# The small blocks' gathers, scatters and summing matmul on 128 rows instead of 32

## The chip, the cores and the metric

The kernel runs on one core of a Trainium2 chip. The metric is the device time of one execution in microseconds. The profile is of one further execution.

## The reference

Three layers follow one another. The first is a linear recurrence over 768 time steps: for each of 4 batches and 8 heads a complex state of 48 x 48 is multiplied by a normalised decay, a key-value product is added, and a query reads it. Its output, seen as 3072 tokens of 384 numbers, goes through a dense layer, and then through a layer of 8 experts, of which each token takes one:

```
h = max(max(x @ w1, x @ w2), x @ w3);  x1 = h @ w_out            # dense layer
expert_idx = argmax(cosine(x1, expert_emb) / tau)                # router
out[mask] = gate[mask] * (max(x1[mask] @ w1[e], 0) @ w2[e])      # mask: the tokens of expert e
```

## The kernel before

Phase 1 (up to about 593 us) computes the recurrence and the dense layer in 12 units of 256 tokens, from a recorded list of operations that a planner in the kernel (class `Recorder`) orders; its lines all appear as L299. The dense layer's output rows go to `x1d` in HBM, from which phase 2 fetches them by token number.

Phase 2 is the expert layer, and the change lies in it. Tokens of one expert are packed into blocks of 128 rows. A column of `self.src` (one number for each of 128 partitions) holds the token numbers of a block, a column of `self.dst` the output rows, a column of `self.gate_of` the gates. Where a row of a block is empty, `late_route` (L1141 to L1145) writes 0 into `src` and 4096 into `dst`; a scatter is told that only rows below 3072 exist (`bounds_check`). The main loop of `phase2` goes over `STEPS`, 14 of them (two single blocks, then 11 pairs of blocks and one more single one, 25 blocks in all). A step k does, in program order: the gather of the rows of step k+2 (L1174), the loads of the next step's expert weights on SP's queue (L1168, L1169), their splitting into a high and a low part by ACT and DVE (`prep`, L1195 to L1205), the two halves of the first matmul (`mm1`, L1243; ACT and DVE evict into `hhi` and `hlo`, L1247 and L1248), the next step's transposes (L1220 to L1226), the second matmul (`mm2`, L1259), the gated copy to `yo` (L1263) and the scatter of each block to `out` (L1265).

An expert with few tokens left over gets a small block of at most 32 rows (`MT`). There are 5 of them (`MINI`), woven into five of the steps (`WITH`) by the generator `small`. A small block loads its weights (L1279, L1280), gathers its 32 rows (L1282), transposes them (L1288), computes the hidden layer in four quarters laid out over 4 x 32 output partitions (L1295), and after the second matmul (L1310) has four partial sums on partitions 0 to 31, 32 to 63, 64 to 95 and 96 to 127. One matmul with `self.four` adds them (L1315): `four` is 128 x 32 and has a one where the partition's number modulo 32 is the column's. ACT applies the gates (L1317) and GpSimd scatters 32 rows (L1318).

```
1282  g.indirect_dma_start(out=xg[:MT], ..., in_offset=IndirectOffsetOnAxis(ap=self.src[:MT, i:i + 1], axis=0), ...)
1315  t.matmul(ps[:MT], self.four, part, start=True, stop=True)
1317  s.activation(y[:MT], ps[:MT], AF.Copy, scale=self.gate_of[:MT, i:i + 1])
1318  g.indirect_dma_start(out=self.io["out"], in_=y[:MT], ..., ap=self.dst[:MT, i - KE:i - KE + 1], ...)
1346  self.four = pool.tile([128, MT], F32, name="four")
1347  nc.vector.tensor_reduce(self.four, self.ident.rearrange("p (j r) -> p r j", r=MT), axis=AX.X, op=ALU.add)
```

`four` is made on DVE before the first step of the loop. `self.mask` is a 128 x 128 tile of phase 1 (the causal mask of the recurrence, read at L594); phase 2 reads it once more, at L856, in the routing of the last tokens. That routing, `late_route`, is written into step 1 (`LATE`), runs on DVE for the most part and ends with `src` and `dst` of all later blocks (L1142, L1145) and with some flags (L1417 to L1425). The gathers of the blocks from step 4 on, and of all small blocks, need its `src`.

In phase 2 the framework, not the kernel, orders the instructions of each engine at compile time, by their place in the program, by what they wait for, and by its own estimate of times. Each engine then runs its queue in that order. An indirect DMA is issued by GpSimd (POOL in the profile).

Of the kernel before, what the change touches and what calls it, by code (L numbers as in the profile page):

```python
# [9 lines left out]
F32 = mybir.dt.float32  # L10
# [4 lines left out]
AF = mybir.ActivationFunctionType  # L15
ALU = mybir.AluOpType
AX = mybir.AxisListType
# [21 lines left out]
KE, KP = 2 * PE, 2 * (PE + PL)  # L39
NBLK = KP + SG  # L40
MT, MINI = 32, 5
# [272 lines left out]
class Prog:  # L314
# [954 lines left out]
    def small(self, pool, mp, pg, m):  # L1269


        nc = self.nc
        t, v, s, g = nc.tensor, nc.vector, nc.scalar, nc.gpsimd
        i, KD, KF, Q = NBLK + m, DM // 128, FF2 // 128, FF2 // 4
        e = nc.values_load(self.mtab[0:1, m:m + 1], engines=[ET.SP], min_val=0, max_val=E - 1,
                           skip_runtime_bounds_check_because="a count of 8 comparisons, of which one fails")
        w1 = mp.tile([128, KD, FF2], F32, tag="w1m", bufs=1, name=f"w1m{m}")
        w2 = mp.tile([128, KF, DM], F32, tag="w2m", bufs=1, name=f"w2m{m}")
        nc.sync.dma_start(w1, self.io["w21"][bass.ds(e, 1)].rearrange("a p (k f) -> p (a k) f", f=FF2))  # L1279
        nc.sync.dma_start(w2, self.io["w22"][bass.ds(e, 1)].rearrange("a p (k f) -> p (a k) f", f=DM))  # L1280
        xg = pool.tile([128, DM], F32, tag="xg", bufs=4, name=f"xgm{m}")
        g.indirect_dma_start(out=xg[:MT], out_offset=None, in_=self.x1d,  # L1282
                             in_offset=bass.IndirectOffsetOnAxis(ap=self.src[:MT, i:i + 1], axis=0),
                             bounds_check=NT - 1, oob_is_err=False)
        yield
        px = pg.tile([128, KD, MT], F32, tag="px", bufs=2, name=f"pxm{m}")
        for k in range(KD):
            t.transpose(px[:, k], xg[:MT, k * 128:(k + 1) * 128], self.ident[:MT, :MT])  # L1288
        x = pool.tile([128, KD, MT], F32, tag="xT", bufs=2, name=f"xm{m}")
        s.copy(x, px)  # L1290
        yield
        ph = pg.tile([128, Q], F32, tag="ph", bufs=3, name=f"phm{m}")
        for k in range(KD):
            for j in range(4):
                t.matmul(ph[j * MT:(j + 1) * MT], x[:, k], w1[:, k, j * Q:(j + 1) * Q], start=k == 0, stop=k == KD - 1,  # L1295
                         skip_group_check=True)
        h = mp.tile([128, Q], F32, tag="hm", bufs=1, name=f"hm{m}")
        s.activation(h, ph, AF.Relu)
        yield
        pt = pg.tile([128, 2, 128], F32, tag="px", bufs=2, name=f"pt{m}")  # L1300
        for c in range(2):
            t.transpose(pt[:, c], h[:, c * 128:(c + 1) * 128], self.ident)
        hT = mp.tile([128, 2, 128], F32, tag="hT", bufs=1, name=f"hT{m}")
        v.tensor_copy(hT, pt)
        yield
        py = pg.tile([128, DM], F32, tag="py", bufs=2, name=f"pym{m}")
        for c in range(2):
            for j in range(4):
                r = slice(j * MT, (j + 1) * MT)
                t.matmul(py[r], hT[:, c, r], w2[:, 2 * j + c], start=c == 0, stop=c == 1, skip_group_check=True)  # L1310
        part = pool.tile([128, DM], F32, tag="yo", bufs=3, name=f"part{m}")
        s.copy(part, py)
        yield
        ps = pg.tile([128, DM], F32, tag="py", bufs=2, name=f"psm{m}")
        t.matmul(ps[:MT], self.four, part, start=True, stop=True)  # L1315
        y = pool.tile([128, DM], F32, tag="yo", bufs=3, name=f"ym{m}")
        s.activation(y[:MT], ps[:MT], AF.Copy, scale=self.gate_of[:MT, i:i + 1])  # L1317
        g.indirect_dma_start(out=self.io["out"], in_=y[:MT], in_offset=None,  # L1318
                             out_offset=bass.IndirectOffsetOnAxis(ap=self.dst[:MT, i - KE:i - KE + 1], axis=0),
                             bounds_check=NT - 1, oob_is_err=False)  # L1320
        yield

    def phase2(self):
        tc, nc = self.tc, self.nc
        with ExitStack() as ctx:
            regs = tc.queue_regs(depth=QD, engines=[ET.SP, ET.Activation, ET.DVE], name="wr")
            qp = ctx.enter_context(tc.tile_pool(name="wq", bufs=1, reuse_waits="tile"))
            q1 = qp.queue([128, 3072], F32, regs=regs, name="q1", contiguous=True)
            q2 = qp.queue([128, 3072], F32, regs=regs, name="q2", contiguous=True)
            pg = ctx.enter_context(tc.tile_pool(name="pg2", bufs=2, space=PSUM, reuse_waits="tile"))  # L1330
            pool = ctx.enter_context(tc.tile_pool(name="m2", bufs=1, reuse_waits="tile"))
            wq = ctx.enter_context(tc.tile_pool(name="ws", bufs=1, reuse_waits="tile"))

            late_ctx = ctx.enter_context(ExitStack())
            rp = late_ctx.enter_context(tc.tile_pool(name="rtp", bufs=1, reuse_waits="tile"))
            load, gather, prep, share, transpose, mm1, mm2, st = self.moe2(pool, wq, pg, regs, q1, q2)
            late = self.late_route(rp, pg)
            gather(*STEPS[1])
            load(0)
            first = prep(*STEPS[0])  # L1340
            for _ in range(2):
                next(first)
            last = NS - SPARE
            few = iter(())

            self.four = pool.tile([128, MT], F32, name="four")
            nc.vector.tensor_reduce(self.four, self.ident.rearrange("p (j r) -> p r j", r=MT), axis=AX.X, op=ALU.add)
            for k, (i, n) in enumerate(STEPS[:last]):
                if k + 2 < last:
                    gather(*STEPS[k + 2])  # L1350
                p, after = iter(()), k + 1 < last
                if k == 0:

                    share(*STEPS[:2])
                    p = first
                elif after:
                    load(k + 1)
                    p = prep(*STEPS[k + 1])
                if k + 1 in WITH:

                    small = self.small(pool, mp, pg, WITH.index(k + 1))
                    next(small)
                next(p, 0)
                mm1(i, n, 0)

                for _ in few:
                    pass
                if k in WITH:
                    few = small_now
                    next(few)  # L1370
                if k + 1 in WITH:
                    small_now = small
                next(p, 0)
                mm1(i, n, 1)
                next(few, 0)
                next(p, 0)
                if after:
                    transpose(*STEPS[k + 1])
                for b in range(n):
                    next(p, 0)  # L1380
                    mm2(i, n, b)
                    next(few, 0)
                for _ in p:
                    pass
                for _ in range(LATE.count(k)):
                    next(late)
                if k == LATE[-1]:
                    late_ctx.close()
                    mp = ctx.enter_context(tc.tile_pool(name="mp", bufs=1, reuse_waits="tile"))

    def run(self):
# [287 lines left out]
```

## Time and profile before

| what | us |
|---|---|
| median of 3 runs | 886.02 |
| lowest, highest | 885.44, 891.13 |
| profiled execution | 888.17 |
| its span in the trace | 886.4 |

The span is what lies between the first and the last instruction of the trace; 1.77 us of the profiled execution lie around it. All stretches and times below are in us from the span's start. Busy shares are those of one engine; PE is TensorE's matmuls, PEld its weight loads, which overlap them.

### The profile page before, as it was taken

The page shows a single profiled execution, that of the slowest core. Times are in us where ns is not written, and L with a number is a line of the kernel's source. Part 1 is how long each engine was busy: PE and PEld are TensorE (multiplying, and loading weights), DVE is VectorE, ACT ScalarE, POOL GpSimd, SP SyncE. Part 2 cuts the span into 40 slices and gives each one's busy share as a digit, 9 for nine tenths or more (in the row PEclk, how much of TensorE's full clock was granted, in tenths as well). Part 3 has the DMA queues.
Part 4 walks back from the last instruction along what each step waited for, and adds up shares of the span by engine and source line. Part 5 has one row for each costly group of instructions (what it writes and reads, how often), then busy time and mean ns, then how long its engine had stood idle before and what let it go on. Part 6 is the DMA issues. An engine that isn't in the chain of part 4 may idle for free. (4 is left out here: it accounts for less than half of the span.)

```text
span 886.4 us, 17517 instructions
## 1 busy us (share of the span) xinstructions
PE 812.3 (92%) x6741; PEld 710.8 (80%) x6741; DVE 643.4 (73%) x1371; ACT 434.6 (49%) x918; POOL 124.1 (14%) x194
## 2 busy tenths in 40 slices
PE   0877999999999999999999999998969899989991
PEld 0755697979898887979797988888959788888991
DVE  5998898899888899889898853548966454555610
ACT  7897545435554436454445341137327455455420
POOL 5521100010000000000001000021032222222110
PEclk9889899999999999999999999999989999999996
DMA  8641153443716071715254250050065756665000
GB/s 309 252 116 28 38 133 92 98 130 60 171 31 165 25 175 36 154 51 138 89 101 112 47 109 4 19 206 25 21 251 199 295 205 251 246 251 180 14 20 21
DMA packets 38669, 107.93 MB, mean 122 GB/s; under 512 B 5299, under 2 KB 26833, under 8 KB 35504
## 3 DMA queue, kind: packets, MB, share of 16 engines
q1 hardware_dynamic: 30032, 77.15, 30.6%
q0 software_dynamic: 8000, 28.78, 9.8%
q8 instruction: 55, 0.90, 0.4%
q10 hardware_dynamic: 544, 0.79, 0.3%
q14 instruction: 38, 0.31, 0.1%
HBM read 97.19 MB, written 9.88 MB: 121 GB/s over the span
## 5 line engine op out<-in xcount | busy, mean ns | idle before, releaser
L299 PE MATMUL ph<-xhi,whi 128*128 128x256 f32 x648 | 117.2, 289 | 0.4 <-DVE slotgate L299 0.4
L299 PE MATMUL ph<-xhi,wlo 128*128 128x256 f32 x648 | 112.9, 283 | 0.0
L299 PE MATMUL ph<-xlo,whi 128*128 128x256 f32 x648 | 112.9, 283 | 0.0
L299 PEld LDWEIGHTS ph<-xhi,whi 128*128 128x128 f32 x648 | 93.5, 192 | 2.9 <-PE slots L299 0.5
L299 PEld LDWEIGHTS ph<-xlo,whi 128*128 128x128 f32 x648 | 93.2, 192 | 0.0
L299 PEld LDWEIGHTS ph<-xhi,wlo 128*128 128x128 f32 x648 | 93.1, 192 | 0.0
L1243 PE MATMUL ph<-xh,w1s 128*128 128x256 f32 x264 | 76.2, 289 | 1.6 <-DVE hlo L1248 1.6
L1205 DVE TENSOR_TENSOR w2l<-queue_q_buf,w2h 128x768 fp32r<-128x768 f32 x52 | 47.8, 954 | 37.2 <-ACT w2h L1204 36.9
L1243 PE MATMUL ph<-xh,w1l 128*128 128x256 f32 x264 | 74.7, 283 | 0.0
L1243 PE MATMUL ph<-xl,w1s 128*128 128x256 f32 x264 | 74.6, 283 | 0.0
L1259 PE MATMUL py<-w2h,hhi 128*128 128x384 f32 x200 | 69.8, 349 | 4.7 <-ACT hhi L1247 4.7
L1259 PE MATMUL py<-w2h,hlo 128*128 128x384 f32 x200 | 68.8, 345 | 5.1 <-DVE hlo L1248 4.9
L299 PE MATMUL px<-wo,h 128*128 128x392 f32 x192 | 71.2, 502 | 0.0
L1248 DVE SCALAR_TENSOR_TENSOR hlo<-ph,hhi 128x512 fp32r<-128x512 f32 x50 | 34.3, 686 | 48.7 <-ACT hhi L1247 48.7
L1259 PE MATMUL py<-w2l,hhi 128*128 128x384 f32 x200 | 68.3, 341 | 0.0
L299 DVE TENSOR_TENSOR h<-ph,h 128x512 f32<-128x512 f32 x72 | 49.5, 688 | 25.1 <-PE ph L299 22.9
L299 PE MATMUL py<-at,v 128*64 128x128 f32 (+1 forms) x576 | 57.1, 279 | 0.4 <-DVE at L299 0.4
L299 PE MATMUL pa<-S 112*128 112x128 f32 x384 | 52.6, 280 | 4.8 <-ACT kt L299 4.8
L299 PEld LDWEIGHTS pa<-S 112*128 112x128 f32 x384 | 49.3, 194 | 9.7 <-ACT kt L299 5.5
L1243 PEld LDWEIGHTS ph<-xh,w1s 128*128 128x128 f32 x264 | 50.5, 191 | 7.0 <-issue 5.0
L1247 ACT ACTIVATE hhi<-ph 128x512 fp32r<-128x512 f32 x50 | 29.7, 598 | 49.7 <-PE ph L1243 49.5
L299 PE MATMUL py<-S,Ts 112*64 112x128 f32 x480 | 51.5, 291 | 0.0
(404 smaller groups left out, 1832.3 us busy)
## 6 DMA issues: line engine op xcount, KB each, us to landing
queue_q_buf<-w SPq DMA_DIRECT2D x26, 1536.0 KB
S<-QK SPq DMA_DIRECT2D x46, 289.1 KB
QKr<-qk SPq DMA_DIRECT2D x11, 768.0 KB
X<-a SPq DMA_DIRECT2D x10, 768.0 KB
w1m<-w SPq DMA_DIRECT2D x5, 1536.0 KB
w2m<-w SPq DMA_DIRECT2D x5, 1536.0 KB
v<-v POOLq DMA_DIRECT2D x24, 288.0 KB
x1d<-x1s SPq DMA_DIRECT2D x20, 192.0 KB
```

The source lines that it names most:

```text
L299: getattr(getattr(self.nc, c[0]), c[1])(*c[2], **c[3])
L1205: v.tensor_sub(lo, bv[:, c], hi.bitcast(F32))
L1243: t.matmul(ph[:, f], a, b, start=o == 0, stop=o == len(ops) - 1)
L1247: s.activation(hi, ph, AF.Relu).ins,
L1248: v.scalar_tensor_tensor(lo, ph, 0.0, hi.bitcast(F32), op0=ALU.max, op1=ALU.subtract).ins]
L1259: t.matmul(py, a[:, f, r], c[:, k % 4], start=o == 0, stop=o == 3 * KF - 1)
```

## The change

The gather and the scatter of a small block take all 128 rows of their index column instead of the first 32, and so does the gated copy between them. For that, the summing matmul yields 128 rows: `four` becomes 128 x 128, with zeros in its columns 32 to 127. It has no tile of its own any more: it lies in `self.mask`, which GpSimd sets to zero after the late routing's second part in step 1, and of which DVE then fills columns 0 to 31 by the same reduction as before. The reduction ahead of the loop and the 128 x 32 tile go.

```diff
-        g.indirect_dma_start(out=xg[:MT], out_offset=None, in_=self.x1d,
-                             in_offset=bass.IndirectOffsetOnAxis(ap=self.src[:MT, i:i + 1], axis=0),
+        g.indirect_dma_start(out=xg, out_offset=None, in_=self.x1d,
+                             in_offset=bass.IndirectOffsetOnAxis(ap=self.src[:, i:i + 1], axis=0),
                              bounds_check=NT - 1, oob_is_err=False)
...
-        t.matmul(ps[:MT], self.four, part, start=True, stop=True)
+        t.matmul(ps, self.four, part, start=True, stop=True)
         y = pool.tile([128, DM], F32, tag="yo", bufs=3, name=f"ym{m}")
-        s.activation(y[:MT], ps[:MT], AF.Copy, scale=self.gate_of[:MT, i:i + 1])
-        g.indirect_dma_start(out=self.io["out"], in_=y[:MT], in_offset=None,
-                             out_offset=bass.IndirectOffsetOnAxis(ap=self.dst[:MT, i - KE:i - KE + 1], axis=0),
+        s.activation(y, ps, AF.Copy, scale=self.gate_of[:, i:i + 1])
+        g.indirect_dma_start(out=self.io["out"], in_=y, in_offset=None,
+                             out_offset=bass.IndirectOffsetOnAxis(ap=self.dst[:, i - KE:i - KE + 1], axis=0),
                              bounds_check=NT - 1, oob_is_err=False)
...
-            self.four = pool.tile([128, MT], F32, name="four")
-            nc.vector.tensor_reduce(self.four, self.ident.rearrange("p (j r) -> p r j", r=MT), axis=AX.X, op=ALU.add)
...
                 if k == LATE[-1]:
                     late_ctx.close()
+                    self.four = self.mask
+                    nc.gpsimd.memset(self.four, 0.0)
+                    nc.vector.tensor_reduce(self.four[:, :MT], self.ident.rearrange("p (j r) -> p r j", r=MT), axis=AX.X,
+                                            op=ALU.add)
```

## Rows read from the trace of the kernel before

**Rows 1.** Part 1 of the page, busy us, share of the span, instructions

```profile
PE 812.3 (92%) x6741; PEld 710.8 (80%) x6741; DVE 643.4 (73%) x1371; ACT 434.6 (49%) x918; POOL 124.1 (14%) x194
```

**Rows 2.** Three stretches: length, PE, PEld, DVE, ACT, POOL busy, clock, DMA share, GB/s

```profile
606.00:651.00 45.00, 43.23 (x329) 42.40 (x327) 39.40 (x118) 21.36 (x31) 4.00 (x4) 1.00 0.07 22
651.00:664.00 13.00, 6.03 (x27) 5.20 (x28) 6.08 (x19) 0.96 (x2) 6.85 (x6) 0.74 0.98 406
664.00:869.00 205.00, 196.72 (x1453) 178.72 (x1451) 97.72 (x115) 99.61 (x150) 46.80 (x44) 1.00 0.49 181
```

**Rows 3.** Timeline of PE: start, duration, instruction, idle before it and its releaser

```profile
660.40 0.90 PE L1220 MATMUL pxg<-ident,xg 128*128 128x128 f32 x3 [6.80 <-DMA xg<-x1d,srcrow]
```

**Rows 4.** Timeline of POOL, 618 to 742 us

```profile
618.57 1.00 POOL L1265 DMA_INDIRECT out<-yo,srcrow  x1 [8.92 <-ACT yo L1263]
...
652.30 2.16 POOL L1174 DMA_INDIRECT xg<-x1d,srcrow  x1 [14.47 <-DVE dstrow L1145]
...
740.56 0.96 POOL L1282 DMA_INDIRECT xgm<-x1d,srcrow  x1 [0.30 <-PE py L1259]
```

**Rows 5.** Four lines' own views, indirect DMAs on POOL: ns min/median/max, first and last start

```profile
L1282 POOL DMA_INDIRECT xgm<-x1d,srcrow x5: 920/952/1907, 661.6 to 820.2; - x5
L1174 POOL DMA_INDIRECT xg<-x1d,srcrow x24: 1006/1032/2502, 577.0 to 801.0; - x24
L1318 POOL DMA_INDIRECT out<-ym,dstrow x5: 882/894/900, 695.3 to 856.1; - x5
L1265 POOL DMA_INDIRECT out<-yo,dstrow x19: 982/1000/1623, 684.0 to 869.7; - x19
```

**Rows 6.** Page part 3, bytes moved in HBM

```profile
HBM read 97.19 MB, written 9.88 MB: 121 GB/s over the span
```

**Rows 7.** Chain that ended last, in time: start, us, what (DMA: issue to landing)

```profile
849.45 2.59 DMA out<-yo,dstrow
...
856.08 3.16 DMA out<-ym,dstrow
...
864.81 4.12 DMA out<-yo,dstrow
```

**Rows 8.** Timeline of PE, 738 to 750 us

```profile
746.96 0.37 PE L1288 MATMUL pxm<-ident,xgm 32*128 32x32 f32 x3
```

**Rows 9.** Groups by line and form, 575 to 887 us: busy us, mean ns, idle before

```profile
L299 PE MATMUL px<-wo,h 128*128 128x392 f32 x16 | 5.4, 492 | 0.0
...
L1315 PE MATMUL psm<-part,four 128*32 128x384 f32 x10 | 4.2, 498 | 0.0
...
L299 PEld LDWEIGHTS px<-wo,h 128*128 128x128 f32 x16 | 3.0, 190 | 1.9
...
L1315 PEld LDWEIGHTS psm<-part,four 128*32 128x32 f32 x10 | 0.7, 107 | 0.7
```

**Rows 10.** The same view: the gated copies on ACT

```profile
L1263 ACT ACTIVATE yo<-py,slotgate 128x384 f32<-128x384 f32 x25 | 14.6, 582 | 46.4 <-PE py L1259 38.4 <-issue 6.3 <-ACT w2h L1204 1.6
...
L1317 ACT ACTIVATE ym<-psm,slotgate 32x384 f32<-32x384 f32 x5 | 2.9, 573 | 0.8 <-PE psm L1315 0.8
```

**Rows 11.** Timeline of DVE, 580 to 662 us

```profile
580.21 0.39 DVE L1347 TENSOR_REDUCE four<-ident 128x32 f32<-128x128 f32 x1 [0.34 <-issue]
586.88 0.69 DVE L299 TENSOR_TENSOR h<-ph,h 128x512 f32<-128x512 f32 x1 [6.28 <-PE ph L299]
...
595.84 0.18 DVE L1417 TENSOR_SCALAR inrange<-ss 128x24 f32<-128x24 f32 x1
...
607.52 0.28 DVE L856 TENSOR_TENSOR upper<-mask,ident 128x128 f32<-128x128 f32 x1
...
651.64 0.18 DVE L1145 CAST dstrow<-empty 128x31 int32<-128x31 f32 x1
651.78 1.76 DVE L1199 TENSOR_TENSOR w1l<-queue_q_buf,w1s 128x1536 fp32r<-128x1536 f32 x1
...
661.85 0.56 DVE L1226 TENSOR_TENSOR xl<-pxg,xh 128x384 fp32r<-128x384 f32 x1 [5.76 <-ACT xh L1225]
```

**Rows 12.** Groups of POOL over the whole span: a memset of one 128 x 128 tile

```profile
L299 POOL MEMSET ones<- 128x128 f32 x1 | 0.2, 206 | 0.0
```

## The prediction

> **What bounds the kernel now.** I read the page's busy shares first, then three stretches of phase 2, then the timelines of PE, POOL and DVE, and at last the chain. The reader is to see that TensorE carries the span: it is busy 92% of it, POOL 14% [rows 1]. In the stretch where the small blocks run, 664 to 869 us, PE is busy 196.72 of 205 us, POOL 46.80, and the DMA engines move for 0.49 of the time [rows 2]. There, whatever POOL or a DMA takes longer costs nothing as long as PE does not stand waiting for it. Two places before that are different. From 606 to 651 us the late routing fills DVE, 39.40 of 45 us, so 5.6 us are idle there [rows 2]. Its end, the write of `dst` at 651.64, releases POOL's gather at 652.30 [rows 4, 11]; and PE then stands 6.80 us, until that gather has landed at 660.40 [rows 3], while the DMA share is 0.98 [rows 2]. So what is added to DVE inside the late routing can be paid in full; what is added to POOL or to the transfers of the small blocks is hidden at nearly every place.
>
> **The change part by part.**
>
> *Issuing 128 rows instead of 32.* The issue of a small gather takes 952 ns at the median, of a full one 1032; of a small scatter 894, of a full one 1000 [rows 5]. That is 5 x 0.080 + 5 x 0.106 = 0.93 us more on POOL, which has 158 us idle in that stretch. What stands behind each on POOL is a gather two steps ahead or a scatter; none is needed within a tenth of a microsecond. I take 0; the worst is 0.93, were each of them waited for.
>
> *Moving 128 rows.* Each transfer grows from 32 x 1536 B = 49 KB to 197 KB, so the ten move 1.47 MB more, half of it read and half written. Bytes written now are 9.88 MB [rows 6]: that is 24 x 128 rows of `x1d` and (25 x 128 + 5 x 32) rows of `out`, 1536 B each, to the last digit, so empty rows of a full block are counted although `dst` puts them out of bounds. I therefore expect the 96 added rows to be moved, or counted, like those. From issue to landing, a scatter of 32 rows took 3.16 us, two of 128 rows 2.59 and 4.12 [rows 7]: the change lies between -0.57 and +0.96 us for each. The scatters are waited for by nobody before the next scatter: the last small one lands at 859.24 and the next issue is at 864.81, 5.57 us later, so +0.96 is covered. A gather is waited for by PE's transposes. The closest pair is the third small block: issue at 740.56 [rows 4], transposes at 746.96 [rows 8], 6.4 us apart; and there PE did not wait. With landing times like those above (up to 4.12) it still would not; the gather of 652.30 took 8.1 us until PE had it, under a DMA share of 0.98 [rows 2 to 4]. Bounds for this place: 0 and 8.1 - 6.4 = 1.7 us. I take 0.2, near the lower end, since PE does not wait there now and only this one of the five is close.
>
> By the Trainium skill, page "DMA: Bandwidth & Descriptors", section "Anatomy of one DMA — SWDGE (gpsimd) path", a DMA from GpSimd costs about 2.0 us plus its bytes over 436 GB/s, which makes 128 rows 0.34 us later than 32 (an estimate from that page). That lies inside the measured -0.57 to +0.96 and would, fully exposed at the one close gather, make the sum 0.54 instead of 0.4.
>
> *The summing matmul.* Its moving side stays 384 columns; the weights grow from 32 to 128 columns. Ten instructions (two for each block) are busy 4.2 us, 0.42 each; the nearest row with 128 weight columns has 16 in 5.4 us, 0.34 each, at 392 columns [rows 9]. Their mean durations are alike, 498 and 492 ns. So the wide form could gain 10 x 0.08 = 0.8 us. On the other side its weight loads take 190 instead of 107 ns, 10 x 0.083 = 0.83 us if none is hidden beside the matmul before it [rows 9]. Bounds -0.8 and +0.83; I take 0, the middle, since the durations are equal.
>
> *The gated copy.* 32 rows take 573 ns, 128 rows 582 [rows 10]: 0.05 us for five, off PE's path. 0.
>
> *The reduction moves.* Ahead of the loop it took 0.39 us at 580.21, and 6.28 us of idle DVE follow [rows 11]; to take it away there gives 0. Now it comes after a memset of 128 x 128 on POOL, 206 ns in the nearest row [rows 12], which in turn waits for the last reader of `mask`, L856 at 607.52 [rows 11]. Queued on DVE inside the late routing, it puts its 0.39 us ahead of 651.64, and the wait of PE grows by as much; queued after it, it falls into the 5.76 us idle before 661.85 [rows 11] and costs nothing. Behind it on DVE stand the evictions `hlo`, for which PE waits. Bounds 0 and 0.39; I take 0.2. What needs `four`, the first summing matmul, comes 30 us later.
>
> *Sum.* 0 + 0.2 + 0 + 0 + 0.2 = +0.4 us. On the profiled execution, 888.17, that makes 888.6; that execution lies 2.15 us above the median 886.02, so I forecast 886.4 for a median.
>
> **The rivals.**
>
> *The order falls differently and the stall before 660 us shrinks (faster).* The order on an engine is made at compile time and is not the program's: L1417, the last part of the late routing, runs at 595.84, 11.7 us ahead of L856 in its first [rows 11]. Other costs and a moved reduction can shift it. If PE got as much of the second matmul ahead of the waiting transposes as the stall is long, up to 6.8 us would go [rows 3]: 879.6. For it: PE still had matmuls of that step to do, behind the transposes. Against it: nothing here makes the gather itself earlier, and the DMA share of 0.98 stays.
>
> *DVE stands behind POOL (slower).* The reduction now waits for POOL, whose queue in that time holds scatters that wait for ACT and PE: the one of 618.57 stood 8.92 us [rows 4]. If the memset is queued behind it and the reduction right after L856, near 609, DVE stands from there until 619.6 + 0.2, some 10.5 us, and with it the whole late routing and PE's evictions. DVE has 5.6 us idle in that stretch to make up for it; it decides from a blockade longer than these. The price lies between 10.5 - 5.6 = 4.9 and 10.5 us, 890.9 to 896.5. For it: POOL and DVE had no such tie here before. Against it: the memset is ready at 607.8, while POOL idles 8.92 us waiting for that scatter, so an order by readiness puts it first.
>
> *The close gather lands late.* Beside the 1.7 us at the third small block there is the issue itself: the longest ones of three lines took 1623, 1907 and 2502 ns [rows 5], and that of 652.30, with 2.16 us, begins while DVE's L1199 runs its 1.76 us [rows 4, 11]. The 1907 is a small gather. Hit there too, the block is 1.7 + 1.1 = 2.8 us late: 889.2. Against it: the long issues are there already with 32 rows. The Trainium skill, page "SBUF — State Buffer", section "Who interferes with whom", says that a DVE instruction with two SBUF inputs contends with a GpSimd instruction that reads SBUF, and that the loser stands until the other is done; these rows agree.
>
> *The added rows cost nothing because they are not moved.* If out-of-bounds rows are dropped at the issue, the scatters stay as they are and only the gathers grow: the sum is 0.2 to 0.3 and the time the same, 886.3.
>
> **How the numbers follow.** A measurement of this kernel can tell about 1% from no change, 8.9 us: 877.2 and 894.9 are the bounds. Chances: the forecast, 884.5 to 888.5, 0.62; shrunk stall, 879.6 to 884.5, 0.13, of it a little below 877.2 with other shifts; DVE behind POOL 0.11, a half of it above 894.9; late gather, 888.5 to 891, 0.09; rows not moved 0.05. The three runs of before alone span 885.44 to 891.13, so I leave the range at 880.5 to 893.5: that leaves out the far ends of the two order cases. Faster by over 1%: 0.04, from the second case; slower: 0.08, 0.05 from the third and 0.03 for an order that falls worse than before's at the stall; within: 0.88.
>
> **What would show it.** Right: HBM read 97.9 and written 10.6 MB; ten indirect issues of 1.0 us; five summing matmuls of the 128*128 form with about the same busy time; the reduction on DVE with no wait longer than the memset; the wait before 660 us between 6.5 and 7.5. Wrong: an idle stretch of several us on DVE ahead of the reduction, with POOL as its releaser; a wait of PE for a small gather; the first full gather of the late blocks released much before or after 652; or an order of the second matmul and the transposes around 653 to 661 us that differs from before's.

## The result, and the profile after

The changed kernel took 878.34 us (median of 4 executions, 874.65 to 879.0) and the kernel before 886.53 (median of 4, 885.44 to 891.13). The ratio is 0.9883, with a 95% interval of 0.9857 to 0.991: 1.2% faster, clear of no change. The forecast was 886.4, with a range from 880.5 to 893.5; the result lies 2.2 us below the low end. The profiled execution took 878.75 us with a span of 876.9, against 888.17 and 886.4 before: 9.5 us less span.

First the terms of the forecast, in the views that answer to the rows shown of before. The page's bytes and three groups by line and form:

```profile
HBM read 97.92 MB, written 10.62 MB: 124 GB/s over the span
```

```profile
L1315 PE MATMUL psm<-part,mask 128*128 128x384 f32 x10 | 4.0, 487 | 0.0
L1317 ACT ACTIVATE ym<-psm,slotgate 128x384 f32<-128x384 f32 x5 | 2.9, 583 | 0.2
L1315 PEld LDWEIGHTS psm<-part,mask 128*128 128x128 f32 x10 | 1.5, 192 | 0.0
```

The two lines' own views of the small blocks' gathers and scatters (ns min/median/max):

```profile
L1282 POOL DMA_INDIRECT xgm<-x1d,srcrow x5: 1000/1046/1996, 661.3 to 821.7; - x5
...
L1318 POOL DMA_INDIRECT out<-ym,dstrow x5: 982/984/992, 696.3 to 859.0; - x5
```

The three stretches, with the columns of [rows 2]:

```profile
606.00:651.00 45.00, 43.23 (x329) 42.40 (x327) 39.83 (x120) 21.14 (x31) 4.22 (x5) 1.00 0.07 23
651.00:664.00 13.00, 6.20 (x27) 5.38 (x28) 6.28 (x19) 0.96 (x2) 7.20 (x6) 0.70 0.98 407
664.00:869.00 205.00, 198.90 (x1453) 183.19 (x1451) 97.41 (x114) 99.09 (x149) 52.24 (x44) 0.98 0.49 185
```

None of this shows a gain. The bytes are those that were forecast, the issues take the longer form's time, the matmul and the copy cost what they cost before [rows 6, 9, 10], and PE is about as full in each stretch as in [rows 2]. POOL's timeline says the same up to its last instruction:

```profile
858.96 0.99 POOL L1318 DMA_INDIRECT out<-ym,dstrow  x1 [7.03 <-issue]
866.00 0.98 POOL L1265 DMA_INDIRECT out<-yo,dstrow  x1 [6.04 <-ACT yo L1263]
870.90 0.98 POOL L1265 DMA_INDIRECT out<-yo,dstrow  x1 [3.92 <-ACTq L1435]
```

The last scatter is issued at 870.90. In the kernel before it was this row of the same timeline:

```profile
869.71 0.98 POOL L1265 DMA_INDIRECT out<-yo,dstrow  x1 [3.91 <-ACTq L1433]
```

So the changed kernel reaches its last scatter 1.2 us *later*, and ends 9.5 us earlier. The whole gain lies behind the last scatter, in some 16 us of span in which no engine is counted as busy. What fills them is on POOL's own queue (POOLq), in the views of two lines: the branch around the last, rarely needed part of the program, and the end of the program. Before (ns min/median/max, first and last start):

```profile
L1433 POOLq INC_SWDGE_SEM  x1: 2540/2540/2540, 873.4 to 873.4; - x1
...
L1675 POOLq DRAIN  x3: 46/103/9619, 875.9 to 886.1; - x3
```

After:

```profile
L1435 POOLq INC_SWDGE_SEM  x1: 400/400/400, 874.5 to 874.5; - x1
...
L1677 POOLq DRAIN  x3: 46/103/881, 874.9 to 876.6; - x3
```

The INC_SWDGE_SEM lost 2540 - 400 = 2140 ns, the longest DRAIN 9619 - 881 = 8738 ns: 10.88 us together. Less the 1.19 us by which the last scatter is later, that leaves 9.7 us, and the span is 9.5 shorter. Everybody else stands at the program's last barrier meanwhile, as SP's waits from 860 us on show, first before, then after (what was waited for, us in total, times, longest):

```profile
SPq L1675 <- PEq L1675: 9.2, 2, 8.6
```

```profile
SPq L1677 <- PEq L1677: 0.7, 2, 0.5
```

The name of the releaser misleads here: PE's sequencer is only one more that waits for POOL. The end of the program in the kernel before shows it (first and last start): ACT's queue is there at 869.2 us, and it and PE's go on only after POOL's semaphore of 885.6.

```profile
L1675 POOLq EVENT_SEMAPHORE  x4: 17/17/17, 885.6 to 886.3; - x4
...
L1675 ACTq DRAIN  x2: 8/10/13, 869.2 to 885.8; - x2
...
L1675 PEldq EVENT_SEMAPHORE  x2: 51/51/51, 885.7 to 886.3; - x2
```

In the rest of the text *tail* means the INC_SWDGE_SEM and the longest DRAIN together: 12.16 us before, 1.28 after.

### The profile page after: what moved, and what is told of

Its sections match the earlier page's. It is cut to its first block, busy times and chain, and to the rows that moved or that the text cites. A ratio compares the mean times of both kernels' runs of the same rounds, so it can differ in the third digit from the quotient of the medians.

```text
span 876.9 us, 17518 instructions
## 1 busy us (share of the span) xinstructions
PE 813.1 (93%) x6741; PEld 714.6 (81%) x6741; DVE 643.4 (73%) x1371; ACT 434.1 (50%) x918; POOL 133.1 (15%) x195
## 5 line engine op out<-in xcount | busy, mean ns | idle before, releaser
L1259 PE MATMUL py<-w2h,hlo 128*128 128x384 f32 x200 | 70.9, 355 | 3.3 <-DVE hlo L1248 3.0
```

What stands on the lines that cost most here:

```text
L1259: t.matmul(py, a[:, f, r], c[:, k % 4], start=o == 0, stop=o == 3 * KF - 1)
```

## The experiments

The question was what the tail depends on. "Ratio" is the time to that of the kernel before, from 4 to 10 executions of each experiment and 17 to 25 of before beside it.

**Which part of the change is it?** Two candidates stood on record: the order or the place of the tile (L), since `four` now lies in `mask` and the instructions around it moved; and each 32-row DMA that is left being dear at the end (R), so that the tail shrinks in proportion to how many are widened, or only the gathers or only the scatters being so. A total that has to be passed was put on record only after these had failed. Three kernels take the change apart. In the first, of the changed kernel, `four` stays in `mask` and all else goes back to 32 rows:

```diff
-        g.indirect_dma_start(out=xg, out_offset=None, in_=self.x1d,
-                             in_offset=bass.IndirectOffsetOnAxis(ap=self.src[:, i:i + 1], axis=0),
+        g.indirect_dma_start(out=xg[:MT], out_offset=None, in_=self.x1d,
+                             in_offset=bass.IndirectOffsetOnAxis(ap=self.src[:MT, i:i + 1], axis=0),
...
-        t.matmul(ps, self.four, part, start=True, stop=True)
+        t.matmul(ps[:MT], self.four[:, :MT], part, start=True, stop=True)
...
-        s.activation(y, ps, AF.Copy, scale=self.gate_of[:, i:i + 1])
-        g.indirect_dma_start(out=self.io["out"], in_=y, in_offset=None,
-                             out_offset=bass.IndirectOffsetOnAxis(ap=self.dst[:, i - KE:i - KE + 1], axis=0),
+        s.activation(y[:MT], ps[:MT], AF.Copy, scale=self.gate_of[:MT, i:i + 1])
+        g.indirect_dma_start(out=self.io["out"], in_=y[:MT], in_offset=None,
+                             out_offset=bass.IndirectOffsetOnAxis(ap=self.dst[:MT, i - KE:i - KE + 1], axis=0),
```

> The changed kernel with every gather, copy and scatter of the small blocks back at 32 rows; four stays in the mask tile, zeroed by GpSimd after the late routing. At the end POOL's semaphore instruction and its drain took 2.54 + 9.62 = 12.16 us before and 0.40 + 0.88 = 1.28 after. Theory R (rows): each of the ten 32-row DMAs leaves GpSimd about 1.1 us to do at the end: 12 us again, time 886 to 887. Theory L (layout and order: the moved tile, the memset, the other instruction addresses at the end): 1.3 us, time 878.

Measured: 887.7 us, ratio 1.0018 (0.9998 to 1.0038). The same two lines of POOL's queue:

```profile
L1435 POOLq INC_SWDGE_SEM  x1: 2540/2540/2540, 876.1 to 876.1; - x1
```

```profile
L1677 POOLq DRAIN  x3: 46/103/9619, 878.6 to 888.8; - x3
```

To the nanosecond the tail of before. Order and place are out, and the moved reduction with its memset costs nothing that is clear of noise.

The second is the kernel before with the five gathers alone at 128 rows, the third the changed kernel with the five gathers back at 32, so that the scatters alone are wide. The edit of the second (that of the third is its reverse, and stands first in the diff above):

```diff
-        g.indirect_dma_start(out=xg[:MT], out_offset=None, in_=self.x1d,
-                             in_offset=bass.IndirectOffsetOnAxis(ap=self.src[:MT, i:i + 1], axis=0),
+        g.indirect_dma_start(out=xg, out_offset=None, in_=self.x1d,
+                             in_offset=bass.IndirectOffsetOnAxis(ap=self.src[:, i:i + 1], axis=0),
```

> The kernel before with the five small gathers alone on 128 rows; scatters, the summing matmul and four as before. Theory R, in proportion: five 32-row DMAs are left, 12.16 - 5 x 1.09 = 6.7 us on POOL at the end, time 881 to 882. If only 32-row scatters leave something: 12 us, 886.5; if only gathers: 1.3 us, 876 to 878. Theory L: 12 us, 886.5, since the order is that of before.

> The changed kernel with the five small gathers back at 32 rows; scatters on 128. Theory R, in proportion: 6.7 us at the end, time 882 to 884. If only scatters leave something: 1.3 us, 878; if only gathers: 12 us, 887 to 889. Theory L: 1.3 us, 878.

Measured: the gathers alone 888.22 us, ratio 1.0026 (1.0003 to 1.0049); the scatters alone 886.39, ratio 0.9995 (0.9972 to 1.0019). Both have the long tail, 2540 and 9619 ns. A tail in proportion to the narrow DMAs would have been near the middle, 6.7 us, in both, and were only gathers or only scatters dear, one of the two would be short. Half of the change gives nothing of the gain; both halves give all of it.

**How sharp is the edge?** The changed kernel with only its last small scatter back at 32 rows:

```diff
+        r = MT if m == MINI - 1 else 128
...
-        g.indirect_dma_start(out=self.io["out"], in_=y, in_offset=None,
-                             out_offset=bass.IndirectOffsetOnAxis(ap=self.dst[:, i - KE:i - KE + 1], axis=0),
+        g.indirect_dma_start(out=self.io["out"], in_=y[:r], in_offset=None,
+                             out_offset=bass.IndirectOffsetOnAxis(ap=self.dst[:r, i - KE:i - KE + 1], axis=0),
```

> The changed kernel with the last small block's scatter alone back at 32 rows. Theory R, in proportion: one 32-row DMA, 1.3 + 1.1 = 2.4 us at the end, time 879 to 880. If a single DMA of another size is enough (a threshold): 12 us, 888. Theory L: 1.3 us, 878.

Measured: 877.88 us, ratio 0.9892 (0.9849 to 0.9935), and a tail that is even a little shorter:

```profile
L1436 POOLq INC_SWDGE_SEM  x1: 380/380/380, 873.3 to 873.3; - x1
```

```profile
L1678 POOLq DRAIN  x3: 46/103/799, 873.7 to 875.4; - x3
```

One narrow scatter at the very end does not bring any of the tail back, against the 2.4 us of R and the 12 us of a single DMA being enough. What L forecast came, but L had failed in the first experiment. And 20 ns and 82 ns less are a hint: they look like one unit of something that is counted.

**Narrow DMAs, or a total?** If narrow DMAs are the trouble (N), only widening them helps. If a total is, any added rows will do. So the kernel before keeps all its ten 32-row DMAs and gets six full gathers that nobody reads, ahead of step 12's work; the second form has twenty:

```diff
+                if k == 12:
+                    for x in range(6):
+                        xg = pool.tile([128, DM], F32, tag="xg", bufs=4, name=f"xgd{x}")
+                        nc.gpsimd.indirect_dma_start(out=xg, out_offset=None, in_=self.x1d,
+                                                     in_offset=bass.IndirectOffsetOnAxis(ap=self.src[:, KE + x:KE + x + 1], axis=0),
+                                                     bounds_check=NT - 1, oob_is_err=False)
```

> The kernel before, with all ten small DMAs at 32 rows, and six more gathers of 128 rows that nobody reads, issued by POOL in step 12. Theory C (count): the end of POOL is long (2.54 + 9.62 us) until its queue has carried enough rows, and short (0.4 + 0.9 us) beyond; the ten wide DMAs of the change add 960 rows, with 480 it was long, with 864 short; six gathers add 768. It then takes 0.4 + 0.8 us and the time is 876 to 879. Theory N (narrow): more than one 32-row DMA makes the end long: 12.2 us, time 886 to 888.

> As the run with six more gathers, with twenty. Theory C, if what is left at the end grows again from the point where it fell (0.380 + 0.799 us with 864 rows more, 0.400 + 0.881 with 960, so 0.102 us for 96 rows): 2560 rows give 1.28 + 16.7 x 0.102 = 3.0 us, time 878 to 881. Theory C without growth: 1.3 us, 876 to 879. Theory N: 12.2 us, 886 to 890.

Measured with six: 875.01 us (1 us under the forecast), ratio 0.9891 (0.9851 to 0.9931), tail 380 and 799 ns. The kernel does six useless gathers more and is 1.1% faster: N falls. With twenty: 887.58, ratio 0.9997 (0.9974 to 1.002). The time is the one that N forecast, but the tail is short:

```profile
L1439 POOLq INC_SWDGE_SEM  x1: 681/681/681, 881.3 to 881.3; - x1
```

```profile
L1681 POOLq DRAIN  x3: 46/103/2030, 882.0 to 884.6; - x3
```

Its tail is 2.71 us, 9.4 less than before's. But POOL issues the added gathers one after another until 863, with scatters behind them, and ACT, which needs a `yo` buffer back, stands for 12.09 us:

```profile
866.48 0.57 ACT L1317 ACTIVATE ym<-psm,slotgate 32x384 f32<-32x384 f32 x1 [12.09 <-DMA out<-yo,dstrow]
```

```profile
877.78 0.98 POOL L1265 DMA_INDIRECT out<-yo,dstrow  x1 [2.70 <-ACTq L1439]
```

The last scatter is 8.1 us later than before's 869.71, and the gain is spent. The added DMAs are not free here, since others are queued behind them.

**What is counted?** The tails so far fit one rule: POOL keeps a record of the DMAs that it has issued; at the end INC_SWDGE_SEM takes 200 ns + 20 ns for each one on record and the DRAIN 64 ns + 81.67 ns; and at some total the record is cleared of all but the newest. For the kernel before, which never clears it, the rule asks for (2540 - 200) / 20 = 117 DMAs. The part of the profile on DMA issues has them: 24 loads of `v`, 33 other loads of phase 1, 25 + 5 gathers and 25 + 5 scatters, 117. Some of its lines (tile, queue, operation, count, KB each):

```profile
v<-v POOLq DMA_DIRECT2D x24, 288.0 KB
rwlo<-w POOLq DMA_DIRECT2D x9, 384.0 KB
rwhi<-w POOLq DMA_DIRECT2D x8, 384.0 KB
...
xg<-x1d,srcrow POOLq DMA_INDIRECT x25
...
out<-yo,dstrow POOLq DMA_INDIRECT x19
```

The next two kernels test this from the other side. Both are the changed kernel with loads of `v` moved from POOL to SP; the first moves the last four of 24, the second all:

```diff
-        q.gpsimd.dma_start(vt, self.io["v"][ct])
+        (q.sync if ct >= 20 else q.gpsimd).dma_start(vt, self.io["v"][ct])
```

The second has `ct >= 0`.

> The changed kernel, where the last four loads of v (128 rows each) are issued by SP instead of POOL: 512 rows fewer on POOL's queue, so 448 more than before, and no 32-row DMA. Theory C: long again, 12.2 us, time 886 to 889. Theory N: 1.3 us, time 877 to 879.

> The changed kernel with all 24 loads of v on SP: 3072 rows fewer on POOL's queue, 2112 fewer than before. Theory C with a length that is set by how many rows the queue has carried since some point: it differs from 12.16 us; with a fixed long case: 12.2 us, 886 to 890. Theory N: 1.3 us, 877 to 880.

Measured: with four fewer 887.01 us, ratio 1.0004 (0.9987 to 1.0021), with none left 888.02, ratio 1.0022 (0.9997 to 1.0048). Both have the long tail again, shorter than before's by just the DMAs that are gone, 113 and 93 in place of 117. The two lines of each, four fewer first:

```profile
L1435 POOLq INC_SWDGE_SEM  x1: 2460/2460/2460, 874.2 to 874.2; - x1
```

```profile
L1677 POOLq DRAIN  x3: 46/103/9292, 876.7 to 886.6; - x3
```

```profile
L1435 POOLq INC_SWDGE_SEM  x1: 2060/2060/2060, 877.6 to 877.6; - x1
```

```profile
L1677 POOLq DRAIN  x3: 46/103/7659, 879.7 to 887.9; - x3
```

The whole gain of the change is lost when four loads leave POOL that the changed kernel issues from 468.98 to 520.06, before phase 2 has its first small block. This is what a total that must be passed does; the small blocks are the same in both kernels.

**Rows or bytes?** The last pair puts one DMA into the kernel before, at the top of step 2: a copy from one SBUF tile into `mask`, which nobody reads by then, of 4-byte words that do not lie side by side. The first form copies 8 words on each of 128 partitions, 1024 pieces in 4 KB, the second 2 words, 256 pieces in 1 KB:

```diff
+                if k == 2:
+                    nc.gpsimd.dma_start(self.mask[:, 0:16:2], self.pos128[:, 0:16:2])
```

The second has `0:4:2` on both sides.

> The kernel before, small blocks at 32 rows, and one more copy from POOL after the late routing: 8 separate words on each of 128 partitions, 1024 pieces of 4 bytes, between two tiles that nobody needs. Theory E (entries): POOL's record is emptied but for the last 7 DMAs when about 600 to 700 more pieces than before's have been issued, whatever their bytes. With 1024 more, that falls on the scatter of step 12's second block, fourth from the last: 4 + 7 = 11 DMAs are left, the semaphore instruction takes 200 + 11 x 20 = 420 ns and the drain 64 + 11 x 81.67 = 962 ns; time 875 to 879. Theory B (bytes or packets of the transfers): 4 KB more are nothing, 118 DMAs are left, 2560 and 9701 ns, 886 to 888.

> As the run with 1024 pieces, with 2 words on each partition, 256 pieces. Theory E: too few, 118 DMAs are left on the record: 200 + 118 x 20 = 2560 ns and 64 + 118 x 81.67 = 9701 ns; time 886 to 888. That any copy of this kind empties the record: as with 1024, 875 to 879.

Measured: 1024 pieces give 877.2 us, ratio 0.9877 (0.9846 to 0.9908), 256 give 884.79, ratio 0.9981 (0.9959 to 1.0002). The longest DRAIN of each:

```profile
L1677 POOLq DRAIN  x3: 46/103/962, 874.8 to 876.5; - x3
```

```profile
L1677 POOLq DRAIN  x3: 46/103/9701, 874.1 to 884.4; - x3
```

These are the rule's values for 11 and 118 DMAs (64 + 81.67 x 11 = 962, x 118 = 9701), and the INC_SWDGE_SEM went with them (420 and 2560 ns). One copy of 4 KB in 0.99 us of POOL does what the whole change does, with the small blocks left at 32 rows. The place and the tail of the first form were put on record before it ran. It is the number of pieces that brings the clearing about, and not their bytes: 480 rows more, 737 KB, did not do it in the second and third experiments, and these 4 KB did. Packets are out as well: both copies bring POOL's queue to the same number (before, it was 8000). With 1024 pieces, then with 256 (packets, MB, share of 16 engines):

```profile
q0 software_dynamic: 8032, 28.78, 9.8%
```

```profile
q0 software_dynamic: 8032, 28.78, 9.7%
```

The timeline on POOL with 1024 pieces also shows the place, and the price, of the clearing:

```profile
852.05 0.99 POOL L1265 DMA_INDIRECT out<-yo,dstrow  x1 [4.96 <-ACT part L1312]
857.20 0.90 POOL L1318 DMA_INDIRECT out<-ym,dstrow  x1 [4.16 <-ACT ym L1317]
865.93 0.98 POOL L1265 DMA_INDIRECT out<-yo,dstrow  x1 [7.83 <-ACT yo L1263]
870.86 0.98 POOL L1265 DMA_INDIRECT out<-yo,dstrow  x1 [3.94 <-ACTq L1435]
```

From 852.05 on four DMAs are issued; with the 7 newest of the older ones that makes 11. In the changed kernel the three from 858.96 on make 10, in the fourth and fifth experiments two make 9, in the one with twenty gathers 17 make 24. The DMA at which it happens starts late. In the changed kernel ACT has `ym` ready at 856.62 + 0.58 = 857.20, and the scatter is issued at 858.96, 1.76 us later:

```profile
856.62 0.58 ACT L1317 ACTIVATE ym<-psm,slotgate 128x384 f32<-128x384 f32 x1
```

In the kernel before the same distance was 0.28 us: ACT's `ym` ran from 855.23 for 0.57, and the scatter went at 856.08 [rows 7]. So the clearing takes about 1.5 us once, and the profile puts it down as "issue", a wait for nothing that it shows. With 1024 pieces the releaser of the row at 852.05 hides it: `yo` was ready at 849.71 + 0.58 = 850.29, again 1.76 us earlier.

```profile
849.71 0.58 ACT L1263 ACTIVATE yo<-py,slotgate 128x384 f32<-128x384 f32 x1 [3.88 <-PE py L1259]
```

In the fourth and fifth experiments the scatter at which the count puts the clearing starts 1.77 and 1.84 us after its input. From 840 us on, the other scatters of these four kernels but the very last, and those of the kernel before, start 0.27 to 0.29 us after theirs. Earlier in phase 2 some scatters start late in every kernel, so a late start alone does not show a clearing. In these four kernels the clearing lies in a stretch in which POOL waits for ACT anyway.

**The changed kernel again**, unedited, beside these two:

> The changed kernel once more, beside the run with 1024 pieces: 10 DMAs left, 400 and 881 ns, time 876 to 879 and a ratio of 0.985 to 0.991 to the kernel before. The run with 1024 pieces is expected within 3 us of it.

Measured: 875.19 us (0.8 us under the forecast), ratio 0.9862 (0.9834 to 0.9891), tail 400 and 881 ns. The intervals of this and of the 1024 pieces overlap: neither is shown to be the better one, and the gain of the change stands repeated.

All tails against the rule, in ns; e1 to e11 are the experiments in the order in which they are told. In the rows from 93 up the number on record is counted from the DMA issues; in the others it is read from the INC_SWDGE_SEM, so that there the DRAIN is the test (and the 11 of e9, which was forecast):

```
                    on record   INC: 200+20n, measured   DRAIN: 64+81.67n, measured
before, e1, e2, e3     117         2540, 2540                9619, 9619
e10, 256 pieces        118         2560, 2560                9701, 9701
e7, four fewer         113         2460, 2460                9293, 9292
e8, no v on POOL        93         2060, 2060                7659, 7659
e6, twenty more         24          680,  681                2024, 2030
e9, 1024 pieces         11          420,  420                 962,  962
after, e11              10          400,  400                 881,  881
e4, e5                   9          380,  380                 799,  799
```

**What stays open.** What the record is was only argued. The Trainium skill, page "DMA: Bandwidth & Descriptors", section "SWDGE vs HWDGE vs iDMA", says that GpSimd itself writes the descriptors of its DMAs into rings in SBUF. A ring that runs full, so that GpSimd has to look which DMAs are done before it can go on, would do what is seen: clear the record at a number of pieces, once, at an issue. No run shows the ring itself. Nor is the limit known but from outside: it was not reached by 480 rows more than the kernel before has (the two halves of the change) and was by 768 (the six gathers). Rows alone don't place it exactly. With the twenty gathers 2560 rows are added, and the 16 DMAs behind the clearing have 15 x 128 + 32 = 1952, so it came at 608 more. In the fourth experiment 864 are added, and the clearing falls on the scatter before the last: ahead of these two, 864 - 256 = 608 more had been issued, and it had not yet come. So each DMA seems to count for something beside its rows. A kernel made to count this alone was not tried.

## Why the prediction was wrong

Its mechanism for the stretches that it looked at held nearly everywhere, and the time came from one that it left out.

- *What bounds the kernel* was read from three stretches that end at 869 us [rows 2]. The span was 886.4. The chain [rows 7] was followed to the scatter of 864.81, and the last start in [rows 5] is 869.7; the 16 us behind it were never asked about. There POOL, on which what is added was said to be hidden at nearly every place, alone sets the end. **This is the step that failed**: it priced the added rows by issue and landing and left out what POOL does for its DMAs at the end of the kernel. That term measured -10.88 us. No rival held it either; the one faster rival put the gain at the stall before 660.
- *Issuing 128 rows*: forecast 5 x 0.080 + 5 x 0.106 us on POOL, hidden. Measured 1046 - 952 = 94 and 984 - 894 = 90 ns at the median. At the median it held. In sum POOL was busy 52.24 us from 664 to 869 us after 46.80 [rows 2], 5.44 more where 0.93 was forecast: there are eight issues of 1.47 to 2.59 us in place of four of 1.62 to 2.50. The added rows are not shown to be the reason, since with the small blocks at 32 rows the first experiment had 50.05 us in the same stretch and the one with 1024 pieces 51.26. It was hidden, as forecast. The clearing makes one issue start 1.5 us later.
- *Moving 128 rows*: HBM read and written were forecast as 97.9 and 10.6 MB and came out so; the rival of rows that are not moved falls. The last small scatter landed 2.22 us after its issue (3.16 with 32 rows), 0.94 less where the low bound was 0.57 less. The close gather, the third, came late by 0.59 us where 0.2 was taken and 1.7 was the bound; in PE's timeline:

```profile
748.82 0.34 PE L1288 MATMUL pxm<-ident,xgm 32*128 32x32 f32 x3 [0.59 <-DMA xgm<-x1d,srcrow]
```

  Before, PE did not wait there [rows 8], and a wait of PE for a small gather was one of the signs of being wrong. The wait belongs to the wide form: all seven profiles of kernels with wide gathers or scatters have it, with 0.4 to 0.9 us, and none of the six with both at 32 rows. But the wider gather is not the whole reason: with the gathers alone wide PE waited 0.62 us, and with the scatters alone wide, the gathers at 32 rows, 0.55. The third experiment's row:

```profile
747.71 0.34 PE L1288 MATMUL pxm<-ident,xgm 32*128 32x32 f32 x3 [0.55 <-DMA xgm<-x1d,srcrow]
```

  So the wider scatters, taken as hidden, cost something here too; by what way is open. The term was sized too small, within its bounds. The rival that put 2.8 us on it fails.
- *The summing matmul*: forecast 0 between -0.8 and +0.83; busy 4.0 after 4.2 us, its weight loads 1.5 after 0.7. *The gated copy*: 583 ns where 582 was taken. Both held.
- *The reduction moves*: forecast +0.2. The memset was queued behind a scatter, and DVE waited for it:

```profile
608.52 1.04 POOL L1265 DMA_INDIRECT out<-yo,srcrow  x1 [8.25 <-ACT yo L1263]
609.54 0.24 POOL L1388 MEMSET mask<- 128x128 f32 x1
...
652.22 2.17 POOL L1174 DMA_INDIRECT xg<-x1d,srcrow  x1 [14.47 <-DVE dstrow L1145]
```

```profile
609.81 0.38 DVE L1389 TENSOR_REDUCE mask<-ident 128x32 f32<-128x128 f32 x1 [1.61 <-POOL mask L1388]
```

  The tie of the slower rival is there, but the scatter in front is one that was about to go, so that DVE loses 1.61 us and not 10.5. That is still more than the memset's 0.24, which the prediction had set as the longest wait if it was right. The 5.6 us that DVE had idle in the stretch [rows 2] take that in: the gather that ends the late routing is issued at 652.22, where it was 652.30 [rows 4]. The term is 0.
- *The stall before 660* was 6.80 us [rows 3] and is 6.62, as forecast within 6.5 to 7.5; the faster rival fails:

```profile
660.11 0.90 PE L1220 MATMUL pxg<-ident,xg 128*128 128x128 f32 x3 [6.62 <-DMA xg<-x1d,srcrow]
```

- *The sum to the last scatter* was +0.4 and measured +1.2, in one execution of each. Single executions don't tell that: with the long tail, the last scatter started at 867.93 in the second experiment's and at 872.63 in the first's. The ratios bound it better: the place of the tile alone gave 1.0018, the gathers alone 1.0026, the scatters with the tile's place 0.9995, with intervals that reach from 0.9972 to 1.0049. So each part of the work that the change adds is worth half a per cent at most, none shows a gain, and the gain is the tail's. The gathers alone are slower clear of noise, by at least 0.03% or 0.27 us, a little more than the 0.2 taken for them.

The bound of 1% for what can be told from no change served: -1.2% and the ratios of the experiments fall into two groups, 0.986 to 0.989 and 0.998 to 1.003, and each kernel's tail says to which it belongs, but for the one with twenty gathers, which gives its gain back.

## What to carry to other kernels

Ask of every profile what lies between the last instruction that does work and the end of the span, on the engines' queues as well: here it was 16 us, and 12.16 of them were POOL's, about 0.1 us for each DMA that GpSimd had issued and still had on record. Where the loads of a kernel can go by SP's queue instead, that part falls with their number, if the load itself costs no more there (moving all 24 of `v` took 2.44 us off the long tail, and the last scatter of that kernel was issued at 874.10, 3.2 us later than the changed kernel's, in one execution of each; and against the changed kernel the move was a loss, since the record was no longer cleared). A gain of this kind, or a loss, can come with any edit that adds or takes away GpSimd DMAs or their rows, anywhere in the program; compare the tails before an edit is given the credit, since the next edit can take it back, as four fewer loads did.

## What the hardware showed that was not expected

GpSimd's DMAs are paid for a second time at the end of the kernel: 0.2 us + 0.020 us for each in INC_SWDGE_SEM, 0.06 + 0.0817 in the DRAIN, exact to a few ns over 13 profiles and independent of size. As the tails read, the record is cleared of all but 7 once a number of pieces is passed, for about 1.5 us at one issue, so that more work on GpSimd can make a kernel 1.1% faster. The Trainium skill, page "VectorE: DVE Perf Modes", section "The DRAIN you can't avoid", speaks of a DRAIN around the program of about 12 ns, constant, on all engines; the ones here on POOL took 46, 103 and 799 to 9701 ns (ACT's at the same place 8 to 13), and the measurement decides.
